# Attention of batches 3 to 7 spread over 1.4 instead of 1.6 pairs of a mixer kernel, with a fourth pair by seven products

## The chip, the core and the metric

The kernel runs on one core of a Trainium2 chip. The core has a matrix engine (PE), a vector engine (DVE), a scalar engine for activations (ACT), a general engine (POOL) and an engine that mostly issues DMA transfers (SP). Each takes its instructions in order and waits for the others by semaphores. The metric is the device time of one execution in microseconds; it was 559.47 us before (median of three runs, 558.79 to 559.52).

## What is computed

Normalised attention over 8 batches of 12 heads (448 positions, 64 columns a head), then a low-rank mix over positions, then a two-layer network of 768, 3072 and 768 columns:

```python
q_n, k_n = rmsnorm(q, g_q), rmsnorm(k, g_k)
scores = scale * np.matmul(q_n, k_n.transpose(0, 1, 3, 2))
attn = np.exp(scores - max); attn = attn / (sum(attn) + 1e-09)
x = (attn @ v).transpose(0, 2, 1, 3).reshape(B, S, H * D)

h = x.transpose(0, 2, 1) @ U @ V
u = x + h.transpose(0, 2, 1)
out = u + np.maximum(u @ w_ch1, 0.0) @ w_ch2
```

## The kernel before, in words

**Tiles of positions.** The 8 x 448 positions are 28 tiles of 128. A ring `xr` of ten tiles (`NX`, line 106) holds x, and a ring `ur` of four (`NU`) holds u turned around. Tiles 0 to 2 go through the network together (`mlp_first`), tile 3 alone (`mlp_single`), tiles 4 to 27 by pairs (`mlp_pair`, g = 1 to 12; pair g has tiles 2g+2 and 2g+3).

**A pair.** The first layer (`ph`, line 648) takes 144 products of 256 columns: 24 column blocks of `w1b`, six partial products each. Each bank of results is evicted through `relu` into `hT`, two times of three by ACT (line 430), else by DVE (line 432). The second layer (`po`, line 521) is always made of seven block products in the manner of Strassen and Winograd, 84 products of 384 columns, on sums of blocks of `hT` (DVE, line 529) and of `w2b` (kept in `comb`).

**A late pair.** From pair `LATE` on (10 before) the first layer too is made of seven products (`products_late`, line 572): seven times 36 products of 128 columns. They run in words like `10 50 11 20 60 51 21 70 30 ...`; the first digit is the product, the second which third of the 12 column blocks it makes, and a word is 12 products. Products 1 and 5 open banks of their own; ACT copies product 1's bank into a further bank, to which 6 and 7 add. After 6 a DVE addition (line 609) reads this bank, and after 7 another one (line 611). They need sums of blocks of `w1b`: R1 = V21 + V22, R2 = R1 - V11, R3 = V11 - V21 (written over V21), R4 = V12 - R2, 12 pieces each, all on DVE (line 548), and four sums of u (`sums_u`, into the tile E0). Product 5 uses R1, 6 uses R2, 7 uses R3, 3 uses R4. `held`, in the tile E1, takes intermediate results. So the first late pair can't begin before the last attention has let go of E0 and E1.

**Attention.** Twelve heads of a batch are six head pairs p (48 in all, `NP`). For a head pair: load raw q and k (fp32), squares (ACT, line 236), sums over columns (`reduce`, DVE, line 241), the reciprocal root (`rsqrt`, ACT, lines 246 and 247, for two head pairs at a time), scaling to bf16 (`scale`, POOL, line 256), a transpose by DMA into `qkT` (SP, line 286), then scores (PE, line 304), exponentials (ACT, line 313), the product with v (PE, line 320) and the division by the row sums (DVE, lines 335 to 348). Scores run in sessions of three, eight sessions a batch. Squares are made four head pairs ahead of the scores, scaling and transpose two ahead.

**Raw q and k.** A load covered two head pairs (`load(t)`, four transfers), into one of two buffers `qkL` of 2048 columns. In the steady part it was issued at every second head pair, behind the transpose of the second one.

**The order of the work.** It is all written out by hand. `step` takes the next piece of network work (`fill`) and, each time, one pending DVE sum, or two from the list `slack` when none is pending. `weave` puts attention pieces between, by weights, so that they are spread evenly up to a given place of the network:

```python
for b in range(2, B):
    end = 1.557 + 1.6 * (b - 2)
    weave(fill, stage(end), attention(b))
    weave(fill, stage(end + 0.257), mixing(b))
```

A place of 3.5 is half through pair 3, counted in PE columns; the first layer is the first 0.533 of a pair. Attention of batch 7 so ended at 9.557, just past the first layer of pair 9. `mixing` makes u of a batch and turns it into `ur` by DMA (`turn_u`), which waits for a place in the ring where there is none. At the start of a late pair, what is pending is issued and `slack` is emptied down to 12 pieces; the rest goes on two a step, at the latest ahead of the words of product 7.

Of the kernel before, what the change touches and what calls it, by code (L numbers as in the profile page):

```python
# [10 lines left out]
FP32 = mybir.dt.float32  # L11
BF16 = mybir.dt.bfloat16
# [6 lines left out]
def kernel(  # L19
# [83 lines left out]
    vas = [v[0:SP] for v in vw]  # L103


    NX, NU = 10, 4
    xr = consts.tile([P, NX, dm], BF16, name="xr")
    ur = consts.tile([P, KD, NU * P], BF16, name="ur")
    zero = xr[:, NX - 1]
    qkTs = [consts.tile([P, SQK + 16], BF16, name=f"qkT{i}") for i in range(NQ)]  # L110
    qkL = [consts.tile([P, 2, 2, 2, NJ * D], FP32, name=f"qk{i}") for i in range(2)]
    vL = consts.tile([P, HG, NJ * D], FP32, name="vt")
    part = consts.tile([P, HALF], FP32, name="part")

# [8 lines left out]
    def as_v(x):  # L123
        return x.rearrange("p (h c) -> p h c", h=HG)

    qk_of = {2: spare[:, 0:2048].rearrange("p (a s h c) -> p a s h c", a=2, s=2, h=2)}
    v_of = {0: as_v(slot(4)), 1: as_v(slot(5)), 2: as_v(spare[:, 2048:3072]), 4: as_v(slot(4)), 5: as_v(slot(5)),
            7: as_v(slot(5))}
    for t in range(NT):
        qk_of.setdefault(t, qkL[(t - (t > 2)) % 2])  # L130
        v_of.setdefault(t, vL)

    def setup():
# [62 lines left out]

    def load_pair(eng, t, s, a, hs=slice(0, 2)):
        rows, src = heads((q, k)[s], HG * t + 2 * a + hs.start, hs.stop - hs.start)
        eng.dma_start(qk_of[t][0:rows, a, s, hs], src)

    def load(t):
        for a in range(2):
            for s in range(2):
                load_pair(nc.sync, t, s, a)

    def load_v(t):
        rows, src = heads(v, HG * t, HG)
# [1 line left out]

    def touch(t):  # L210

        nc.vector.memset(qk_of[t][0:1, :, :, 0, 0:1], 0.0)
        nc.vector.memset(v_of[t][0:1, 0, 0:1], 0.0)

    def cast_v(t):
        nc.gpsimd.tensor_copy(vas[t % NV][:, :, :, 0:D], v_of[t][0:SP].rearrange("p h (j d) -> p h j d", d=D))

    def new_sq():
        return norm.tile([P, 2 * 2 * NJ * D], FP32, tag="sq", name="sq", bufs=1)

    def new_qkn():
        return norm.tile([P, NJ, 4, D], BF16, tag="qkn", name="qkn", bufs=2)
# [1 line left out]
    ALL = slice(0, 2)  # L224

    def squares(p, eng="pool", hs=ALL):
        t, a = divmod(p, 2)
        if 2 <= p < 6:
            sqs[p] = w2b[0:SP, 1].rearrange("p k n -> p (k n)").bitcast(FP32)[:, (p - 2) * 1024:(p - 1) * 1024]
        elif p < 16 and p not in sqs:  # L230
            sqs[p] = slot(p % 4 if p > 5 else p)[0:SP]
        elif p not in sqs:
            sqs[p] = new_sq()[0:SP]
        src, dst = qk_of[t][0:SP, a, :, hs], sqs[p].rearrange("p (s h c) -> p s h c", s=2, h=2)[:, :, hs]
        if eng == "act":
            nc.scalar.activation(dst, src, AF.Square)  # L236
        else:
            nc.gpsimd.tensor_tensor(dst, src, src, OP.mult)
# [8 lines left out]
        nc.scalar.activation(rs, rs, AF.Exp, scale=-0.5)  # L247

    def scale(p, pool=False):
        t, a = divmod(p, 2)  # L250
        qkns[p] = new_qkn()[0:SP]
        out = qkns[p].rearrange("p j g d -> p g j d")
        x = qk_of[t][0:SP, a].rearrange("p s h (j d) -> p (s h) j d", d=D)
        rs = rs_of(p).rearrange("p (g j) -> p g j ()", j=NJ)
        for g in (slice(0, 2), slice(2, 4)) if p >= 12 else (slice(0, 4),):
            (nc.gpsimd if p >= 12 or pool else nc.vector).tensor_tensor(  # L256
                out[:, g], x[:, g], rs[:, g].to_broadcast([SP, g.stop - g.start, NJ, D]), OP.mult)
# [270 lines left out]
    def later(fn, *args):  # L528
        pending.append(lambda: fn(*args))  # L529

    LATE = 10
    wq = w1b.rearrange("p (d i) (k j n) -> p j d k i n", d=2, j=2, n=P)
    Q = KH // 2
    V11, V12, V21, V22 = ([wq[:, j, d, k] for k in range(Q)] for j in range(2) for d in range(2))
# [5 lines left out]
    def pieces(tile_, names, dtype=FP32):  # L540
        x = tile_.rearrange(names)
        x = x.bitcast(BF16) if dtype == FP32 else x
        n = x.shape[1] // (KD // 2 * P)
        return [x[:, i * KD // 2 * P:(i + 1) * KD // 2 * P].rearrange("p (i n) -> p i n", n=P) for i in range(n)]

    def spread(fn, outs, xs, ys, op):
        for o, x, y in zip(outs, xs, ys):
            slack.append(lambda o=o, x=x, y=y: fn(o, x, y, op))

    def sums_first():  # L550
        R1.extend(pieces(qkL[1], "p a s h c -> p (a s h c)") + pieces(vw[0], "p h j d -> p (h j d)", BF16))
        spread(nc.vector.tensor_tensor, R1, V21, V22, OP.add)

    def sums_rest():
        qn = [pieces(new_qkn(), "p j g d -> p (j g d)", BF16) for _ in range(2)]
        R2.extend(pieces(qkL[0], "p a s h c -> p (a s h c)") + qn[0])
        R4.extend(pieces(vL, "p h c -> p (h c)") + pieces(new_sq(), "p c -> p c") + qn[1])
        assert [len(x) for x in (R1, R2, R4)] == [Q] * 3
        spread(nc.vector.tensor_tensor, R2, R1, V11, OP.subtract)
        spread(nc.vector.tensor_tensor, R4, V12, R2, OP.subtract)  # L560

    def quarter(u, d, a):
# [71 lines left out]
    def mlp_pair(g):  # L634
# [8 lines left out]
        for k in range(KH // 2 if g < LATE else 0):  # L643
            ph = ps_mm.tile([P, 4, P], FP32, tag="mm", name="ph")
            for j in range(2):
                hc, out = 2 * k + j, ph[:, 2 * j:2 * j + 2].rearrange("p a n -> p (a n)")
                for dc in range(KD):
                    nc.tensor.matmul(out, w1b[:, dc, hc * P:(hc + 1) * P], u[:, dc, :],  # L648
                                     start=(dc == 0), stop=(dc == KD - 1))
                if j == 0:  # L650
                    yield 2 * P
            relu(hB[:, 0:4, k, :], ph, k % 3 or g > 8)
            if g == 1 and k in (1, 4, 7, 9):
                later(combine, 12 + (1, 4, 7, 9).index(k))
            if k % 4 == 3:
                sums_h(k // 4)
            yield 2 * P
# [71 lines left out]
    def attention(b):  # L729
# [19 lines left out]
        for p in range(b * 6, b * 6 + 6):  # L749
            t, odd = divmod(p, 2)  # L750
            early = p < 12
            if p == 12:
                add(0, gains, p)
            run(p, 0)
            if p == NP - 4:
                add(0, sums_first)
            elif p == NP - 2:
                add(0, sums_rest)
            if p == 11:
                add(0, touch, 7)  # L760
                add(0, load, 7)
                add(0, load_v, 7)
            elif p >= 13 and p + 3 < NP:
                add(0, reduce, p + 3)
            elif early and odd:
                add(0, rsqrt, p + 1, 2)
                add(0, scale, p + 1)
            elif early and p > 6:
                add(0, scale, p + 1)
            run(p, 1)  # L770
            if not odd and p >= 14 and p + 2 < NP:
                add(0, rsqrt, p + 2, 2)
            if p >= 12 and p + 2 < NP:
                add(0, scale, p + 2)
                add(0, dma_transposes, p + 2)
            if p % 6:
                add(1, values, p - 1, 0)
            if p == 11:
                add(0, reduce, 12)
            if early and not odd:  # L780
                add(0.5, transposes, p + 1)
                if p < 10:
                    add(0, reduce, p + 2)
            if p + 1 < NP and p > 11:
                add(0, gains, p + 1)
            run(p, 2)
            if p % 6:
                add(1, values, p - 1, 1)
            if early and not odd:
                if p < 10:  # L790
                    add(0, reduce, p + 3)
                for a in range(2):
                    if p != 8:
                        add(0, squares, (10 if p == 6 else 12) + a)
            if p >= 12 and t + 2 < NT:
                add(0, squares, p + 4, "act")
            if odd and p > 11:
                if t + 3 < NT:
                    add(0, load, t + 3)
                if t + 2 < NT:  # L800
                    add(0, load_v, t + 2)
            if not odd and t + 1 < NT:
                add(0, cast_v, t + 1)
            run(p, 3)
            if early and odd and p < 11:
                add(1, transposes, p + 1)
            if p == 9:
                add(0, touch, 6)
                add(0, load, 6)
                add(0, load_v, 6)  # L810
# [68 lines left out]
    def head():  # L879
# [15 lines left out]
            return held[key].rearrange("p (s j r) -> p s j r", s=2, j=NJ)  # L895

        def raw0(s):
            return qk_of[0][0:SP, 0, s].rearrange("p h (j d) -> p j h d", d=D)

        def op(name, p, n, how):  # L900
            if name == "sq":
# [100 lines left out]
    with tc.manual_schedule():  # L1002
# [55 lines left out]
        for a in range(2):  # L1058
            reduce(14 + a)
        rsqrt(14, 2)  # L1060
        load(8)
        while at[0] < place("single", 0):
            step(fill)
        def stage(x):
# [1 line left out]
            return begins["ph", g][0] + (x - g) * (begins["ph", g + 1][0] - begins["ph", g][0])  # L1066

        for b in range(2, B):
            end = 1.557 + 1.6 * (b - 2)
            weave(fill, stage(end), attention(b))  # L1070
            weave(fill, stage(end + 0.257), mixing(b))
        while step(fill) is not None:
            pass
# [30 lines left out]
```

## Time and profile before

| | |
|---|---|
| median of three runs | 559.47 us |
| the profiled execution | 559.42 us |
| its span in the trace | 557.6 us |
| granted clock of PE | 0.999 |
| first layer of plain pairs (line 648) | 1296 products of 256 columns |
| second layer (line 521) | 1032 products |
| first layer of late pairs (line 595) | 756 products of 128 columns |
| DVE sums for late pairs (line 548) | 48 |
| exponentials (line 313) | 174.9 us busy on ACT |
| loads of q and k on SP after the first | 44 and 44, median 4.3 and 4.8 us to landing |
| transposes qkT by DMA | 36, median 3.1 us to landing |

A line of the page's groups has the source line, the engine, the operation, the tiles (result, then operands), the shape and the number; then busy time, mean length of one, and idle time of the engine before it with what ended it. A matmul's own length overlaps its neighbours', since products are pipelined; the pace of a row of products is its length in the chain of waits over its number. Windows give for one stretch of the span the busy time of each engine. In a view in order of time the first column is the start, the second the length, and what stands in brackets is the idle time before it and its releaser.

### The profile page before, as it was taken

How to read it: one execution, taken by the hardware profiler on the slowest of the kernel's cores; microseconds unless marked ns; L12 is line 12 of the kernel's file. 1: busy time of each engine (PE TensorE's matmuls, PEld its weight loads, DVE VectorE, ACT ScalarE, POOL GpSimd, SP SyncE). 2: the span in 40 equal slices, each digit the busy share in tenths (PEclk: the TensorE clock that was granted, in tenths of full speed). 3: DMA queues.
4: the chain of work that ended last, by engine and by line, in shares of the span. 5: the costliest groups of instructions: out<-in, count | busy, mean ns of one | idle time of the engine just before them, and what ended most of it. 6: DMA issues, size and time to landing. Idle time of an engine off the chain costs nothing.

```text
span 557.6 us, 13969 instructions
## 1 busy us (share of the span) xinstructions
PE 547.9 (98%) x5796; PEld 387.4 (69%) x5798; DVE 375.3 (67%) x834; ACT 318.1 (57%) x539; POOL 174.0 (31%) x171
## 2 busy tenths in 40 slices
PE   8999999999999999999999999999999999999996
PEld 3665665767768577577676686786776777878785
DVE  6977858388667657755676667556759778565654
ACT  7966640688458653678178654786185731515140
POOL 6964127434153230444244502424134100000000
PEclk9999999999999999999999999999999999999999
DMA  8999997946548553675165651668331403110101
GB/s 277 282 237 241 204 238 203 207 134 179 130 91 166 140 120 111 165 163 145 55 127 152 154 166 45 188 130 168 93 77 37 75 2 85 31 58 2 58 2 57
DMA packets 108447, 72.43 MB, mean 130 GB/s; under 512 B 56688, under 2 KB 105056, under 8 KB 108384
## 3 DMA queue, kind: packets, MB, share of 16 engines
q1 hardware_dynamic: 96800, 61.65, 44.2%
q0 software_dynamic: 11008, 9.44, 10.5%
q8 instruction: 45, 0.74, 0.6%
q10 hardware_dynamic: 576, 0.46, 0.3%
q14 instruction: 18, 0.15, 0.1%
HBM read 56.78 MB, written 11.01 MB: 122 GB/s over the span
## 4 chain that ended last, share of the span: by engine, by line
PE 88%; DVE 5%; ACT 3%; issue 1%; DMA 1%; SPq 1%; POOL 0%; DVEq 0%; POOLq 0%
PE po L521 28%; PE ph L648 24%; PE o L320 8%; PE po L476 5%; PE sc L304 4%; PE ph L595 4%; PE ph L458 3%; PE sc L595 3%; PE sh L304 3%; ACT E L313 2%; PE px L397 1%; DMA qk<-in_k_dram 1%; PE ph L486 1%; DVE hT L529 1%; PE bank L320 1%
## 5 line engine op out<-in xcount | busy, mean ns | idle before, releaser
L648 PE MATMUL ph<-ur,w1b 128*128 128x256 bf16 x1296 | 156.0, 273 | 0.0
L521 PEld LDWEIGHTS <-hT 128*128 128x128 bf16 x1032 | 95.9, 98 | 63.2 <-issue 7.2
L648 PEld LDWEIGHTS <-w1b 128*128 128x128 bf16 x1296 | 121.8, 98 | 25.9 <-issue 10.8
L256 POOL TENSOR_TENSOR qkn<-qk,rms 112x512 bf16<-112x512 f32 (+1 forms) x73 | 83.0, 1157 | 152.4 <-ACT rms L247 111.5
L313 ACT ACTIVATE E<-sc 112x896 bf16<-112x896 f32 x138 | 122.0, 920 | 2.2 <-PE sc L304 2.1
L521 PE MATMUL po<-w2b,hT 128*128 128x384 bf16 (+1 forms) x588 | 104.2, 323 | 0.0
L430 ACT ACTIVATE hT<-ph 128x512 bf16<-128x512 f32 (+1 forms) x101 | 58.9, 586 | 71.1 <-PE ph L648 63.8
L529 DVE TENSOR_TENSOR hT<-hT 128x512 bf16<-128x512 bf16 x144 | 73.2, 527 | 17.3 <-ACT hT L430 15.4
L313 ACT ACTIVATE E<-sh 112x448 bf16<-112x448 f32 x108 | 52.9, 543 | 55.9 <-PE sh L304 55.8
L521 PE MATMUL po<-comb,hT 128*128 128x384 bf16 (+1 forms) x444 | 78.5, 322 | 0.0
L320 PEld LDWEIGHTS <-E 112*128 112x128 bf16 x1536 | 60.7, 98 | 10.2 <-issue 2.9
L694 POOL TENSOR_TENSOR osb<-osb,xr 128x384 f32<-128x384 f32 x12 | 11.9, 992 | 152.5 <-DVE osb L693 147.4
L320 PE MATMUL o<-va,E 112*128 112x65 bf16 x1344 | 57.1, 194 | 0.3 <-DVE hT L432 0.2
L335 DVE RECIPROCAL rec<-o 128x4 f32<-128x4 f32 x84 | 15.0, 179 | 48.8 <-PE o L320 48.6
L432 DVE TENSOR_SCALAR hT<-ph 128x512 bf16<-128x512 f32 (+1 forms) x51 | 33.8, 663 | 19.6 <-PE ph L648 17.2
L241 DVE TENSOR_REDUCE sums<-sq 112x16 f32<-112x1024 f32 x32 | 38.7, 1208 | 4.6 <-ACT sq L236 4.5
L304 PE MATMUL sc<-qkT 64*128 64x448 bf16 x268 | 39.1, 351 | 1.3 <-DVE qkT L275 0.6
L399 DVE TENSOR_TENSOR xr<-px,xr 128x384 bf16<-128x384 f32 x56 | 29.9, 551 | 8.1 <-PE px L397 5.1
L476 PE MATMUL po<-w2b,hT 128*128 128x384 bf16 x192 | 34.5, 326 | 0.1
L236 ACT ACTIVATE sq<-qk 112x1024 f32<-112x1024 f32 x32 | 33.9, 1059 | 0.0
L304 PEld LDWEIGHTS <-qkT 64*128 64x128 bf16 x376 | 14.8, 94 | 25.9 <-issue 15.3
L344 DVE TENSOR_TENSOR xr<-o,rec 128x192 bf16<-128x192 f32 (+1 forms) x96 | 30.8, 331 | 2.9
(154 smaller groups left out, 605.8 us busy)
## 6 DMA issues: line engine op xcount, KB each, us to landing
qk<-in_q_dram SPq DMA_DIRECT2D x44, 256.0 KB, 4.3
qk<-in_k_dram SPq DMA_DIRECT2D x44, 256.0 KB, 4.8
vt<-in_v_dram SPq DMA_DIRECT2D x17, 512.0 KB, 6.0
w1b<-in_moe_w_ch_dram POOLq DMA_DIRECT2D x6, 768.0 KB, 20.6
w2b<-in_moe_w_ch_dram POOLq DMA_DIRECT2D x6, 768.0 KB, 36.6
comb<-in_v_dram SPq DMA_DIRECT2D x5, 512.0 KB, 9.0
out_dram<-osb SPq DMA_DIRECT2D x7, 336.0 KB, 3.1
out_dram<-osb SPq DMA_DIRECT2D x7, 288.0 KB, 2.9
```

What stands on the lines that cost most here:

```text
L236: nc.scalar.activation(dst, src, AF.Square)
L241: nc.vector.tensor_reduce(rs_of(p, of=sums).rearrange("p (s h j) -> p s h j", s=2, h=2)[:, :, hs], sqs[p].rearrange("p (s h j d) -> p s h ...
L256: (nc.gpsimd if p >= 12 or pool else nc.vector).tensor_tensor(out[:, g], x[:, g], rs[:, g].to_broadcast([SP, g.stop - g.start, NJ, D]), OP ...
L304: nc.tensor.matmul(sc[hh][0:n, 0:S], flat[pp, c:c + n], blocks(p)[pp, :, 0], start=True, stop=True)
L313: nc.scalar.activation(dst, src, AF.Exp, scale=float(D) ** 0.5)
L320: nc.tensor.matmul(o[:, i, :], E[:, c:c + P], va[:, hl, kc, :], start=(kc == 0), stop=(kc == NJ - 1))
L430: nc.scalar.activation(out, ph, AF.Relu)
L476: nc.tensor.matmul(po, left(hc), w2b[:, half, hc, :], start=(hc == 0), stop=(hc == KH - 1))
L521: nc.tensor.matmul(bank, left[:, k, :], right[:, k, cols], start=start and k == 0, stop=k == KH // 2 - 1, skip_group_check=not start)
L529: pending.append(lambda: fn(*args))
L595: nc.tensor.matmul(to[:, j * P:(j + 1) * P], left[4 * n + j][:, i], right[:, i], start=m in (1, 5) and j == 0 and i == 0, stop=i == KD // ...
L648: nc.tensor.matmul(out, w1b[:, dc, hc * P:(hc + 1) * P], u[:, dc, :], start=(dc == 0), stop=(dc == KD - 1))
```

## The change

Six parts, which belong together:

- `LATE` goes from 10 to 9: pair 9 makes its first layer by seven products too. The pair that is evicted by ACT alone becomes pair 8, and pair 8's last sums go from POOL to DVE.
- Batches 3 to 7 end 1.4 instead of 1.6 pairs after one another; batch 7 ends at 8.557 instead of 9.557. Batch 2 keeps its end at 1.557.
- Ten x tiles become twelve.
- Raw q and k are held by head pairs in three buffers of 1024 columns (`qkP`), some early ones in other tiles. In the steady part each head pair's load (two transfers) is issued at head pair p for p + 5, right behind the transpose of p + 2.
- R1 and R2 lie in the three raw buffers, in `vt` and in the `qkn` tiles, and their sums begin at the last head pair but one; R4 lies in `sq` and in parts of E0 and E1, and its sums are put on the list when batch 7's attention is woven in, behind R3's.
- The tile of zeros for the first warming products is x tile 10 instead of 9.

```diff
-    NX, NU = 10, 4
+    NX, NU = 12, 4
-    zero = xr[:, NX - 1]
+    zero = xr[:, 10]
-    qkL = [consts.tile([P, 2, 2, 2, NJ * D], FP32, name=f"qk{i}") for i in range(2)]
+    qkP = [consts.tile([P, 2, 2, NJ * D], FP32, name=f"qk{i}") for i in range(3)]
...
+    sq0 = as_qk(new_sq())
+    raw = {0: qkP[0], 1: qkP[1], 2: qkP[2], 3: as_qk(slot(3)), 4: as_qk(spare[:, 0:1024]),
+           5: as_qk(spare[:, 1024:2048]), 6: qkP[0], 7: qkP[1], 8: qkP[2], 9: sq0, 10: qkP[0], 11: qkP[1],
+           12: qkP[2], 13: sq0}
+    for p in range(14, NP):
+        raw[p] = qkP[(p + 1) % 3]
...
+    def load_one(p):
+        for s in range(2):
+            load_pair(nc.sync, p // 2, s, p % 2)
...
     def touch(t):
-        nc.vector.memset(qk_of[t][0:1, :, :, 0, 0:1], 0.0)
+        for a in range(2):
+            nc.vector.memset(raw[2 * t + a][0:1, :, 0, 0:1], 0.0)
...
-    LATE = 10
+    LATE = 9
...
     def sums_first():
-        R1.extend(pieces(qkL[1], "p a s h c -> p (a s h c)") + pieces(vw[0], "p h j d -> p (h j d)", BF16))
+        qn = [pieces(new_qkn(), "p j g d -> p (j g d)", BF16) for _ in range(2)]
+        qk = [pieces(x, "p s h c -> p (s h c)") for x in qkP]
+        R1.extend(qk[0] + qk[1] + qn[0])
+        R2.extend(qk[2] + pieces(vL, "p h c -> p (h c)") + qn[1])
         spread(nc.vector.tensor_tensor, R1, V21, V22, OP.add)
+        spread(nc.vector.tensor_tensor, R2, R1, V11, OP.subtract)
 
     def sums_rest():
-        qn = [pieces(new_qkn(), "p j g d -> p (j g d)", BF16) for _ in range(2)]
-        R2.extend(pieces(qkL[0], "p a s h c -> p (a s h c)") + qn[0])
-        R4.extend(pieces(vL, "p h c -> p (h c)") + pieces(new_sq(), "p c -> p c") + qn[1])
+        U = KD // 2 * P
+        R4.extend(pieces(new_sq(), "p c -> p c") + pieces(Ew[0][:, 4 * U:9 * U], "p c -> p c", BF16)
+                  + pieces(Ew[1][:, 2048:2048 + 2 * U], "p c -> p c", BF16))
-        spread(nc.vector.tensor_tensor, R2, R1, V11, OP.subtract)
         spread(nc.vector.tensor_tensor, R4, V12, R2, OP.subtract)
...
-            relu(hB[:, 0:4, k, :], ph, k % 3 or g > 8)
+            relu(hB[:, 0:4, k, :], ph, k % 3 or g == LATE - 1)
...
-            if p == NP - 4:
+            if p == NP - 2:
                 add(0, sums_first)
-            elif p == NP - 2:
-                add(0, sums_rest)
...
                 add(0, scale, p + 2)
                 add(0, dma_transposes, p + 2)
+                if p + 5 < NP:
+                    add(0, load_one, p + 5)
...
             if odd and p > 11:
-                if t + 3 < NT:
-                    add(0, load, t + 3)
                 if t + 2 < NT:
                     add(0, load_v, t + 2)
...
-        load(8)
+        load_one(16)
...
-            end = 1.557 + 1.6 * (b - 2)
+            end = 1.557 + 1.4 * (b - 2)
             weave(fill, stage(end), attention(b))
+            if b == B - 1:
+                sums_rest()
             weave(fill, stage(end + 0.257), mixing(b))
```

## The prediction

> **What bounds the kernel now.** I read the page's busy times, then the chain of waits, then windows over the attention stages, then single engines in order of time.
>
> ```profile
> PE 547.9 (98%) x5796; PEld 387.4 (69%) x5798; DVE 375.3 (67%) x834; ACT 318.1 (57%) x539; POOL 174.0 (31%) x171
> ```
>
> Busy share does not show whether PE runs at its pace, so I read the chain next (start, length, what):
>
> ```profile
> 355.80 3.28 PE ph L648 x30
> ...
> 497.84 2.68 PE ph L595 x48
> ...
> 513.86 11.70 PE po L521 x72
> ```
>
> This gives three paces without a gap: a 256-column product of the plain first layer takes 3.28/30 = 109.3 ns, a 128-column product of the seven-product form 2.68/48 = 55.8 ns, a 384-column second-layer product 11.70/72 = 162.5 ns. A plain pair is thus 144 x 109.3 + 84 x 162.5 = 15.74 + 13.65 = 29.39 us. PE sets the time as long as nobody is late for it.
>
> The windows run over the eight score sessions of batches 2 to 6 (stretch, length, then busy PE, PEld, DVE, ACT, POOL with counts, clock, DMA share, GB/s):
>
> ```profile
> 102.70:139.10 36.40, 35.75 (x438) 26.47 (x436) 26.29 (x52) 31.52 (x53) 16.57 (x14) 1.00 0.69 180
> 158.40:199.50 41.10, 41.10 (x411) 28.62 (x410) 26.04 (x53) 31.91 (x53) 16.52 (x16) 1.00 0.60 130
> 219.90:261.30 41.40, 41.40 (x417) 28.96 (x416) 25.18 (x53) 32.34 (x55) 19.03 (x17) 1.00 0.57 138
> 281.00:321.90 40.90, 40.90 (x417) 29.04 (x416) 27.06 (x60) 32.59 (x55) 18.94 (x17) 1.00 0.59 139
> 342.90:384.00 41.10, 41.10 (x413) 28.63 (x412) 25.45 (x55) 31.75 (x53) 18.61 (x17) 1.00 0.59 130
> ```
>
> Batches 3 to 6 leave PE no idle time, with ACT at 77 to 80%. Batch 2, which the change leaves as it is, is closer packed: ACT 87%, PE idle 0.65 us.
>
> The last views are DVE and PE where the first seven-product pair begins (its first product starts at 469.52):
>
> ```profile
> 470.12 0.55 DVE L722 TENSOR_TENSOR osb<-po,osb 128x384 f32<-128x384 f32 x1
> 470.58 1.15 DVE L548 TENSOR_TENSOR w1b<-w1b 128x384 bf16<-128x384 bf16 x4
> 473.57 0.70 DVE L609 TENSOR_TENSOR ph<-sc,E 128x512 f32<-128x512 f32 x1 [1.84 <-PE sc L595]
> ```
>
> ```profile
> 472.63 0.83 PE L595 MATMUL sc<-E,qk 128*128 128x128 bf16 x12
> 473.30 0.83 PE L595 MATMUL ph<-E,qk 128*128 128x128 bf16 x12
> 473.97 0.83 PE L595 MATMUL ph<-ur,w1b 128*128 128x128 bf16 x12
> 474.64 0.83 PE L595 MATMUL sc<-E,w1b 128*128 128x128 bf16 x12
> ```
>
> The reader is to see that DVE has 1.84 us to spare before L609. L609 adds up bank sc after product 6 of the first third (PE at 472.63), and product 7 (PE at 474.64) writes the same bank, so PE may not start it before L609 has read.
>
> **The change part by part.** The sum starts from the profiled execution's own 559.42 us (span 557.6); the median of the runs is 559.47, so both are the same here.
>
> *Fourth pair by seven products.* It takes 144 products away and puts 7 x 36 = 252 in: 252 x 55.8 = 14.07 us for 15.74, which is -1.67 us on PE. In this kernel PE's time is the span's.
>
> By the Trainium skill ("TensorE: Matmul & The Clock Gate", section "Back-to-back issue gap") this should not pay: it puts a sustained stream of weight load and matmul at about 81 ns for 128 columns, an estimate of 20.4 us for the 252. The trace has 55.8 ns for just this stream in three pairs, and the sum goes by the trace.
>
> *The sums for it.* R1, R2, R3 and R4 are 12 DVE additions each, as before. But R4 now lies in the two E tiles and so waits until batch 7's attention is done, and R3 has by then been put into the list ahead of it. In the built program's order DVE, after pair 8's last eviction (L722 before), has 6 sums of R3 and all 12 of R4 ahead of its first L609; before it had 4 of R3 alone. From the view above: eviction from 470.12, sums from 470.58, 1.15/4 = 0.287 us each. Eighteen take 5.17, so L609 would run from 475.75 to 476.45, and product 7, which stood at 474.64, waits 1.8 us. PE is in order: the rest of the first layer is queued behind it. After that the two are as far apart as before. Bounds: 0, if DVE comes there earlier than I think (it can't come before the eviction, which needs PE's last product, so this takes sums of half the length), and 2.2 us at the 0.35 us of some sums. I take 1.75.
>
> *Batches 3 to 7 at 1.4.* Attention of a batch was spread over 1.6 - 0.257 = 1.343 pairs and gets 1.143: 0.2 x 29.39 = 5.9 us less fill over 8 sessions, 0.73 us each. Sessions stood 41.15/7 = 5.88 us apart in batch 3 (first exponentials at 158.77 and 199.92) and come to about 5.15. Batch 2 has 36.57/7 = 5.22. So batch 2 is what the others become: about 31 us of ACT in 36, 87%. It pays 0.65 us of PE idle, nearly all in one place (PE's next score bank waits for ACT's L430) and while the single tile's evictions, all on ACT, run. A pair gives ACT two evictions of three. Price per batch 0 to 0.65, for five batches 0 to 3.2 us; nearest is the 0 of batches 3 to 6 for most sessions, so I take 0.16 each, 0.8 us. A gain is possible only in batch 7, whose attention has 0.23 us idle now.
>
> *Raw q and k by pairs.* As many loads (two a pair) on SP's queue, but each pair's are issued right behind the transpose of the pair whose buffer they refill. That transpose waits for POOL's scaling, which waits for ACT's rms. At even pairs the squares of the loaded pair on ACT come soon after. From rows: rms ends at 161.02 and the squares one pair-step on begin at 171.30, so 10.3 us, and about 9 us at the new density (1.75 sessions x 0.73 less). Needed: POOL 2.25, SP's transpose 1.25, two load issues 1.03, landing 4.8 (page, k), gaps about 0.2: 9.5 us. ACT would then wait some 0.5 us at about 13 places, with the exponentials of that session queued behind, for which PE's next session waits. ACT at 87% idles 0.13 x 5.15 = 0.67 us a session, so a wait of 0.5 us is mostly covered where that idle time lies next to it. Uncovered it is 13 x 0.6 = 7.8 us. I take 0.8, between 0 and 7.8, nearer to the covered end.
>
> *At nothing.* Twelve x tiles: batch 5's split of one normalisation goes, batch 3 gets one, the same 96 instructions. Two memsets more (60 ns each on DVE), beside PE work. R1 no longer has pieces in va (two sums of 1.1 us there with POOL busy beside); DVE's, not PE's time. Pair 8 instead of pair 9 is evicted by ACT alone and summed by DVE: the same place relative to batch 7's end. The head keeps its order, its loads the same places on SP. Uncovered, any of these is below 0.3 us.
>
> Sum: 559.42 - 1.67 + 1.75 + 0.8 + 0.8 = 561.1 us.
>
> **The rivals.**
> *The gain stands (faster).* The eighteen sums are not late and batches 3 to 7 stay without idle: 559.42 - 1.67 = 557.75. For it: PE idle 0 in four batches and ACT 13% free at the new density. Against it: 18 sums in program order ahead of L609.
> *Gain and sums cancel, the rest is covered (no change).* 559.42 + 0.08 = 559.5. For it: batch 2 idles at one place only; against: every even pair's chain is longer than its time.
> *ACT decides.* From 5.2 us between sessions all five batches pay batch 2's idle: 561.1 + 2.4 = 563.5.
> *Loads decide.* Loads land after ACT is there; half the uncovered price shows: 561.1 - 0.8 + 3.9 = 564.2. It decides once the landing passes 5 us; DMA share is 0.69 in batch 2, 0.6 elsewhere.
> *Weight loads set the pace of the new products.* At the 98 ns of one LDWEIGHTS, 252 take 24.7 us, 9.0 more than the plain layer: 568.4 with nothing else. Three pairs at 55.8 ns speak against it. This is the skill's rule above, made a bound.
> That the fourth pair does not change form is excluded by the built program: 1008 products of 128 columns for 756.
>
> **How the numbers follow.** Forecast 0.34, gain stands 0.21, cancel 0.21, ACT 0.12, loads 0.11, weight loads 0.01. Runs of this kernel can't tell less than 0.2% (1.1 us) from no change, so 558.35 and 560.59 are the limits: faster 0.21; no change 0.21 and the lower edge of the forecast, 0.24; slower the rest, 0.55. The forecast's own range is 560.3 to 562.6. The range of 8 in 10 goes down to the gain standing and up past the two slower cases: 557.6 to 564.8.
>
> **What would show it.** Pair 9's first layer: 252 products at 56 ns with one hole of 1.5 to 2 us ahead of product 7 of its first third, put down to DVE, and 18 sums in a row on DVE just before. No hole: that step was wrong. PE idle in windows over sessions of batches 3 to 7: 0.1 to 0.3 us each; over 0.6, ACT decides. Squares on ACT that wait for a DMA of q or k at even pairs: nought to 0.6 us. If PE loses nothing in these three places, the time is 557.8 and the prediction wrong; if it loses elsewhere (scores waiting for a transpose, x or u tiles late), the accounting is.

## The result, and the profile after

The changed kernel takes 563.97 us (median of four runs, 563.34 to 564.82), against 559.40 before beside it: a ratio of 1.0085 [1.0067, 1.0102], 4.6 us slower. In a second set of runs it took 565.34 (564.00 to 565.59), 1.0095 [1.0078, 1.0113]. The profiled execution took 564.11 with a span of 562.3.

The page's busy times, of after (busy time, share, instructions):

```profile
PE 548.0 (97%) x5906; PEld 388.4 (69%) x5906; DVE 373.7 (66%) x847; ACT 321.4 (57%) x546; POOL 172.4 (31%) x170
```

PE is as busy as before (547.9) in a span 4.7 us longer. So the loss is idle time of PE, which the busy shares cannot place.

The windows over the eight score sessions of batches 2 to 7, of after (stretch, length, then busy PE, PEld, DVE, ACT, POOL with counts, clock, DMA share, GB/s):

```profile
103.40:139.90 36.50, 35.85 (x439) 26.53 (x438) 26.40 (x52) 31.63 (x53) 16.16 (x14) 1.00 0.73 173
159.50:195.20 35.70, 35.17 (x375) 25.21 (x372) 21.76 (x55) 31.40 (x53) 15.08 (x14) 1.00 0.62 149
215.70:252.00 36.30, 35.44 (x366) 24.50 (x362) 21.60 (x48) 29.73 (x51) 18.28 (x16) 1.00 0.57 147
270.00:306.00 36.00, 36.00 (x382) 25.50 (x380) 23.39 (x51) 29.34 (x50) 17.23 (x16) 1.00 0.58 145
326.00:362.00 36.00, 35.89 (x375) 25.00 (x374) 22.22 (x49) 30.16 (x52) 14.61 (x14) 1.00 0.57 146
383.90:420.00 36.10, 34.11 (x356) 23.26 (x353) 19.00 (x50) 26.60 (x48) 14.36 (x12) 1.00 0.39 85
```

The stretches are now 36 us long, as batch 2's was, and ACT is busy 81 to 88% in batches 2 to 6. But PE's idle time does not follow from that: 0.53, 0.86, 0.00, 0.11 and 1.99 us in batches 3 to 7. Batch 7, where ACT has the least to do (74%), loses the most.

The waits of PE, of after (who waits for whom, us in total, times, longest), those that the profile of before does not have:

```profile
PE po L531 <- ACT hT L440: 1.7, 1, 1.7
PE sc L608 <- DVE ph L622: 1.4, 1, 1.4
...
PE ph L661 <- ACT hT L440: 0.7, 1, 0.7
...
PE sc L314 <- ACT qkT L301: 0.5, 1, 0.5
```

(Lines have moved: exponentials are L323, evictions L440, transposes of gains L301, squares L247, scaling L266, the second layer L531, the first layer of plain pairs L661 and of late ones L608, DVE's sums L558 and the addition after product 6 L622.) Four waits stand for most of the loss. Each happens once; they are single places, and not a steady lack of an engine.

*The first* is in pair 7. ACT and PE there, each engine's timeline of after (start, length, engine, line, out<-in, count, and the idle time before it with its releaser):

```profile
383.98 0.97 ACT L323 ACTIVATE E<-sh 112x448 bf16<-112x448 f32 x2
384.82 0.93 ACT L323 ACTIVATE E<-sc 112x896 bf16<-112x896 f32 x1
385.62 0.34 ACT L257 ACTIVATE rms<-sums,eps 112x32 f32<-112x32 f32 x1
386.00 0.23 ACT L258 ACTIVATE rms<-rms 112x32 f32<-112x32 f32 x1
386.13 0.65 ACT L301 ACTIVATE qkT<-qkT,gg 128x448 bf16<-128x448 bf16 x1
386.69 0.90 ACT L323 ACTIVATE E<-sc 112x896 bf16<-112x896 f32 x1
387.49 1.04 ACT L247 ACTIVATE sq<-qk 112x1024 f32<-112x1024 f32 x1
388.43 0.58 ACT L440 ACTIVATE hT<-ph 128x512 bf16<-128x512 f32 x1
```

```profile
385.38 1.95 PE L531 MATMUL po<-w2b,hT 128*128 128x384 bf16 x11
389.07 0.34 PE L531 MATMUL po<-w2b,hT 128*128 128x384 bf16 x1 [1.75 <-ACT hT L440]
```

Batch 7 now begins at place 7.414, with pair 7's first layer ending at 7.533. Its first session puts 4.4 us of work on ACT with no gap in it, and the last eviction of pair 7's first layer stands at the end of that queue. PE, which is in order too, runs the second layer up to the product that needs this eviction and stops for 1.75 us. How little decides this is seen in before: its batch 4 began at the same place of a pair, 3.414, and had the same burst. ACT's timeline of before:

```profile
220.52 0.97 ACT L313 ACTIVATE E<-sh 112x448 bf16<-112x448 f32 x2
221.37 0.93 ACT L313 ACTIVATE E<-sc 112x896 bf16<-112x896 f32 x1
222.16 0.34 ACT L246 ACTIVATE rms<-sums,eps 112x32 f32<-112x32 f32 x1
222.54 0.23 ACT L247 ACTIVATE rms<-rms 112x32 f32<-112x32 f32 x1
222.67 0.65 ACT L291 ACTIVATE qkT<-qkT,gg 128x448 bf16<-128x448 bf16 x1
223.23 0.57 ACT L430 ACTIVATE hT<-ph 128x512 bf16<-128x512 f32 x1
```

There the eviction stood two instructions further ahead, before the next exponential (0.90) and the squares (1.04), and PE lost 0.16 us.

*The second* is the one that was forecast, ahead of product 7 in pair 9. DVE, then PE, of after:

```profile
445.55 0.55 DVE L735 TENSOR_TENSOR osb<-po,osb 128x384 f32<-128x384 f32 x1
446.01 1.70 DVE L558 TENSOR_TENSOR w1b<-w1b 128x384 bf16<-128x384 bf16 x6
447.62 1.43 DVE L558 TENSOR_TENSOR sq<-w1b,qk 128x384 bf16<-128x384 bf16 x5
448.96 1.44 DVE L558 TENSOR_TENSOR E<-w1b,vt 128x384 bf16<-128x384 bf16 x5
450.30 0.63 DVE L558 TENSOR_TENSOR E<-w1b,qkn 128x384 bf16<-128x384 bf16 x2
450.84 0.70 DVE L622 TENSOR_TENSOR ph<-sc,E 128x512 f32<-128x512 f32 x1
```

```profile
449.41 0.83 PE L608 MATMUL ph<-ur,w1b 128*128 128x128 bf16 x12
451.60 0.83 PE L608 MATMUL sc<-E,w1b 128*128 128x128 bf16 x12 [1.36 <-DVE ph L622]
```

Six sums of R3 (into `w1b`) and twelve of R4 (into `sq` and E) run behind the eviction, and only then the addition for which product 7 waits. A word of 12 products starts 0.67 us after the one before; here it is 2.19, so the hole costs 1.52 us.

*The third* is at the start of batch 4: a first-layer product waits 0.70 us for ACT, where again an eviction stood behind a burst of 4.4 us (215.69 to 220.15). The end of the burst on ACT, then PE:

```profile
219.20 1.04 ACT L247 ACTIVATE sq<-qk 112x1024 f32<-112x1024 f32 x1
220.15 1.07 ACT L440 ACTIVATE hT<-ph 128x512 bf16<-128x512 f32 x2
```

```profile
220.78 2.78 PE L661 MATMUL ph<-ur,w1b 128*128 128x256 bf16 x24 [0.70 <-ACT hT L440]
```

*The fourth* is at the start of batch 3: scores wait 0.53 us for ACT to multiply `qkT` with the gains, and ACT had waited 1.37 us for the DMA transpose:

```profile
168.41 0.67 ACT L301 ACTIVATE qkT<-qkT,gg 128x448 bf16<-128x448 bf16 x1 [1.37 <-DMA qkT<-qkn]
169.13 0.36 PE L314 MATMUL sc<-qkT 64*128 64x448 bf16 x2 [0.53 <-ACT qkT L301]
```

The transpose waits for POOL's scaling, and POOL was late. Its timeline of after:

```profile
161.61 1.81 POOL L726 TENSOR_TENSOR osb<-osb,part 128x768 f32<-128x768 f32 x1 [3.97 <-DVE part L719]
163.38 2.05 POOL L266 TENSOR_TENSOR qkn<-qk,rms 112x512 bf16<-112x512 f32 x2
```

A last addition of pair 1 stands ahead of the scaling on POOL, which so begins 1.6 us after ACT's reciprocal root is ready (161.77).

The same addition stood ahead of the same scaling in before (160.87, then 162.64), at no loss. There the scores that needed the transpose began 10.5 us behind the batch's first exponential; here they begin 8.5 us behind it.

What PE lost, place by place, is read from the starts of its products against the paces of the prediction (what a stop costs until the pace is there again, so slightly more than the idle time shown):

| place | us |
|---|---|
| fourth pair by seven products, 252 for 144 | -1.67 |
| start of batch 7, eviction of pair 7 late | +1.91 |
| pair 9, product 7 | +1.52 |
| start of batch 4, eviction of pair 3 late | +0.85 |
| start of batch 3, scaling late | +0.69 |
| eight holes of 0.19 to 0.40 (sum 2.14), for five in before (1.17) | +0.97 |
| the head of this execution was longer | +0.75 |
| sum | +5.0, of 4.7 |

The entry on the head is this execution's own. One and the same early score product starts at 47.49 us in it, at 46.70 in before and at 46.40 in a later profile of the same changed kernel; over all twelve profiles here it starts between 45.88 and 47.49. A difference of two profiled spans therefore has up to 1.6 us of the head in it.

### The profile page after: what moved, and what is told of

Read it like the earlier page. It is cut to its first block, busy times and chain, and to the rows that moved or that the text cites. A ratio compares the mean times of both kernels' runs of the same rounds, so it can differ in the third digit from the quotient of the medians.

```text
span 562.3 us, 14194 instructions
## 1 busy us (share of the span) xinstructions
PE 548.0 (97%) x5906; PEld 388.4 (69%) x5906; DVE 373.7 (66%) x847; ACT 321.4 (57%) x546; POOL 172.4 (31%) x170
## 4 chain that ended last, share of the span: by engine, by line
PE 83%; ACT 6%; DVE 4%; DMA 2%; issue 2%; POOL 1%; SPq 0%; DVEq 0%; POOLq 0%; ACTq 0%
PE po L531 27%; PE ph L661 19%; PE o L330 7%; PE po L486 5%; PE ph L608 5%; PE sc L314 4%; PE sc L608 4%; ACT E L323 3%; PE ph L468 3%; PE sh L314 3%; PE px L407 1%; DMA comb<-in_q_dram 1%; ACT hT L440 1%; ACT sq L247 1%; PE ph L496 1%
## 5 line engine op out<-in xcount | busy, mean ns | idle before, releaser
L661 PE MATMUL ph<-ur,w1b 128*128 128x256 bf16 x1152 | 140.4, 273 | 0.7 <-ACT hT L440 0.7
L531 PEld LDWEIGHTS <-hT 128*128 128x128 bf16 x1032 | 96.1, 98 | 64.8 <-issue 6.1
L661 PEld LDWEIGHTS <-w1b 128*128 128x128 bf16 x1152 | 107.8, 98 | 23.4 <-issue 9.6
L323 ACT ACTIVATE E<-sc 112x896 bf16<-112x896 f32 x138 | 122.0, 920 | 2.2 <-PE sc L314 2.1
L266 POOL TENSOR_TENSOR qkn<-qk,rms 112x512 bf16<-112x512 f32 (+1 forms) x71 | 79.8, 1144 | 133.3 <-ACT rms L258 77.8
L531 PE MATMUL po<-w2b,hT 128*128 128x384 bf16 (+1 forms) x588 | 104.4, 323 | 1.7 <-ACT hT L440 1.7
L440 ACT ACTIVATE hT<-ph 128x512 bf16<-128x512 f32 (+1 forms) x96 | 56.2, 588 | 62.8 <-PE ph L661 55.4
L539 DVE TENSOR_TENSOR hT<-hT 128x512 bf16<-128x512 bf16 x144 | 68.4, 493 | 17.8 <-ACT hT L440 16.2
L323 ACT ACTIVATE E<-sh 112x448 bf16<-112x448 f32 x108 | 52.9, 544 | 45.6 <-PE sh L314 45.4
L531 PE MATMUL po<-comb,hT 128*128 128x384 bf16 (+1 forms) x444 | 77.2, 322 | 0.0
L707 POOL TENSOR_TENSOR osb<-osb,xr 128x384 f32<-128x384 f32 x12 | 14.4, 1198 | 186.1 <-DVE osb L706 177.5
L608 PEld LDWEIGHTS <-w1b 128*128 128x128 bf16 x576 | 34.3, 98 | 3.1 <-issue 1.5
L618 ACT COPY sc<-ph 128x512 f32<-128x512 f32 x12 | 6.8, 570 | 51.1 <-PE ph L608 35.5
L247 ACT ACTIVATE sq<-qk 112x1024 f32<-112x1024 f32 x32 | 33.8, 1057 | 0.5 <-DMA qk<-in_k_dram 0.4
```

Source lines behind the costliest of these rows:

```text
L323: nc.scalar.activation(dst, src, AF.Exp, scale=float(D) ** 0.5)
L440: nc.scalar.activation(out, ph, AF.Relu)
L531: nc.tensor.matmul(bank, left[:, k, :], right[:, k, cols], start=start and k == 0, stop=k == KH // 2 - 1, skip_group_check=not start)
L608: nc.tensor.matmul(to[:, j * P:(j + 1) * P], left[4 * n + j][:, i], right[:, i], start=m in (1, 5) and j == 0 and i == 0, stop=i == KD // ...
```

## The experiments

Each ran beside before on the same chip, and its ratio is to before.

**The order of the sums.** R4 goes on the list ahead of R3 (both in `sums_rest`), and R3's last eight are held back.

```diff
-    pending, slack = [], []
+    pending, slack, kept = [], [], [0]
...
+        spread(nc.vector.tensor_tensor, R3, V11, V21, OP.subtract)
+        kept[0] = 8
...
-        if g == LATE - 1:
-            spread(nc.vector.tensor_tensor, R3, V11, V21, OP.subtract)
...
-            for _ in slack[:2]:
+            for _ in slack[:min(2, max(0, len(slack) - kept[0]))]:
```

> The changed kernel with R4's sums put ahead of R3's on the list and the last eight of R3 kept back until the words of product 7, so that DVE has 10 sums instead of 18 between pair 8's last eviction and the first addition after product 6. My step (the 18 sums cost PE 1.5 us at the start of pair 9): the hole of 1.36 us ahead of product 7 goes, the time falls by 1.4 to 1.6 us, to about 562.5. Rival (the hole belongs to the first late pair in any case, from bank reuse): it stays and the time stays at 564.0.

It took 566.51 (1.0127 [1.0096, 1.0157]): slower than after, a miss. The hole ahead of product 7 was gone, but a larger one had come. PE's timeline of this run:

```profile
444.67 0.83 PE L610 MATMUL ph<-ur,w1b 128*128 128x128 bf16 x12
448.01 0.38 PE L619 MATMUL sc<-w1b 128*128 128x512 bf16 x1 [2.51 <-DVE w1b L558]
```

L619 is a product whose result nobody uses; it opens the bank of product 1's copy. It reads the first 512 columns of `w1b`, blocks of V21 that R3's first sums overwrite, and with R4 first it came behind them. The edit made a wait of its own. So it went in again with this product reading `comb`, and with the held sums let go after the first addition:

```diff
-                    nc.tensor.matmul(Qb[n], w1b[:, 0, 0:P], w1b[:, 0, 0:512], start=True, stop=True)
+                    nc.tensor.matmul(Qb[n], w1b[:, 0, 0:P], comb[:, 0].rearrange("p k n -> p (k n)")[:, 0:512], start=True, stop=True)
...
                 nc.vector.tensor_tensor(Zb[n], Qb[n], keep, OP.add)
+                kept[0] = 0
```

> The first experiment again without the wait that its edit brought in: there PE stood 2.5 us at the matmul that opens the bank of product 6 (it reads columns of w1b that R3's first sums overwrite, and these had come late). It now reads a block of comb, and the rest of R3 is let go after the first addition. 10 sums instead of 18 stand ahead of that addition. My step: no hole over 0.3 us at the start of pair 9, 562.4 for the changed kernel's 564.0. Rival (some other condition holds PE there): a hole of over 1 us stays and the time does not fall.

562.89 (1.0061 [1.0049, 1.0074]). PE's timeline of this run, product 6 and then product 7:

```profile
448.83 0.83 PE L610 MATMUL ph<-ur,w1b 128*128 128x128 bf16 x12
449.50 0.83 PE L610 MATMUL sc<-E,w1b 128*128 128x128 bf16 x12
```

Product 7 follows at the pace. A hole of 0.41 us is left at 451.5, where product 4 waits for the addition after 7, which eight sums of R3 precede. So the hole of 1.52 us came from the order of the eighteen sums, and the mended order leaves 0.41 of it. The median fell by 1.1, which fits; by the intervals it is 1.1 give or take 1.2, so the traces show this and the times alone do not.

**The last eviction of pair 7.** DVE takes it instead of ACT.

```diff
-            relu(hB[:, 0:4, k, :], ph, k % 3 or g == LATE - 1)
+            relu(hB[:, 0:4, k, :], ph, k % 3 and not (g == 7 and k == 11) or g == LATE - 1)
```

> The changed kernel with the last first-layer bank of pair 7 evicted by DVE instead of ACT. The trace has PE waiting 1.75 us there for ACT's eviction, which stands behind 4.4 us of work that the start of batch 7 puts on ACT. If that queue is the cause: the hole goes and the time falls by 1.7 to 1.9 us, to about 562.1. Rival (PE would have waited for batch 7's scores or for ACT's copy of part a moment later anyway): the hole moves, the time falls by less than 0.5 us.

561.50 (1.0039 [1.0019, 1.0059]), 2.5 us below after (give or take 1.5), by one eviction moved; 1.7 to 1.9 were expected. PE's timeline of this run at the place where after has 1.75 us idle:

```profile
385.45 2.11 PE L531 MATMUL po<-w2b,hT 128*128 128x384 bf16 x12
387.50 0.36 PE L314 MATMUL sh<-qkT 64*128 64x448 bf16 x2
```

The twelve products run through. The eviction's place in ACT's queue was the cause, shown.

**Three pairs, closer attention kept** (`LATE = 10`, 1.4 as in the change).

> The changed kernel with LATE back at 10: closer attention, pair buffers and twelve x tiles, but no fourth pair by seven products (and so R4's sums long before pair 10). If the closer attention carries the loss: 1.67 us of gain go, 1.5 us of hole go, the time stays within 0.4 us of the changed kernel's 564.0, and the holes at the starts of batches 3, 4 and 7 are still there. Rival (the fourth pair and its sums carry the loss): close to the 559.4 of before.

564.38 (1.0085 [1.0061, 1.0109]), as slow as after. The waits of PE in this run:

```profile
PE po L531 <- ACT hT L440: 1.8, 1, 1.8
...
PE ph L661 <- ACT hT L440: 0.7, 1, 0.7
...
PE sc L314 <- ACT qkT L301: 0.5, 1, 0.5
```

The same three places, without the one in pair 9. Fourth pair and sums together are worth 563.97 - 559.40 less 564.38 - 559.63, which is -0.2 us, give or take 1.7 by the intervals; the table's -1.67 + 1.52 gives -0.15.

**The buffers alone** (`LATE = 10`, 1.6 instead of 1.4, and R4 ahead of R3 on the list). The first form had the wait of the first experiment in it (2.13 + 0.40 us at the same products), so that its 563.62 (1.0066 [1.0044, 1.0087]) gives no verdict on buffers:

> The changed kernel with LATE at 10 and the attention 1.6 pairs apart, with the sums' order of the first experiment: only the raw pairs in three buffers, their loads behind the transposes, and twelve x tiles are left of the change. If these cost nothing: 559.4 as before, within 0.3 us. If the 0.75 us that the changed kernel lost in the first 13 us of its profile belong to the buffers: 560.2. If the loads come late even at the old spacing: 561 or more, with ACT waiting for q and k.

With the mended order:

```diff
-    LATE = 9
+    LATE = 10
...
-            end = 1.557 + 1.4 * (b - 2)
+            end = 1.557 + 1.6 * (b - 2)
```

> The fourth experiment again with the same mending: raw pairs in three buffers, their loads and twelve x tiles, at 1.6 pairs and with three late pairs. Its profile with the 2.5 us of the edit's own holes was 2.5 us above before. If buffers and loads cost nothing: 559.6, within 0.5 us of before. If they cost what the fourth experiment's median had over its own profile: 561 or more.

559.92 (1.0031 [1.0002, 1.0059]), 0.4 us above before, and its profiled execution 558.91, half a microsecond below before's. The interval is wide, 0.1 to 3.3 us, since two of the eleven executions took 565.7 and 566.8. In the trace every wait of PE of 0.5 us or more stands in before's too, and the mended order's hole of 0.41 is added. So at the old spacing three raw buffers by pairs, their loads and twelve x tiles cost about 0.4 us by the median, and nothing that the trace shows.

**The two other places.** Pair 1's last additions go from POOL to DVE, and DVE evicts one more bank of pair 3.

```diff
-            relu(hB[:, 0:4, k, :], ph, k % 3 or g == LATE - 1)
+            relu(hB[:, 0:4, k, :], ph, k % 3 and not ((g, k) == (3, 7)) or g == LATE - 1)
...
-        if LATE - 1 <= g and not last:
+        if (LATE - 1 <= g or g == 1) and not last:
```

> The changed kernel with two edits at the starts of batches 3 and 4: pair 1's last additions on DVE instead of POOL, so that POOL scales 1.8 us earlier and the transpose for the session at 168 us is there in time; and one bank of pair 3's first layer (block 7) evicted by DVE instead of ACT. If the bursts at batch starts are the cause: the holes of 0.69 and 0.86 us go, the time falls by 1.5 us to 562.4. Rival (something else is late right behind): at least one hole stays over 0.4 us.

561.59 (1.0048 [1.0035, 1.0060]), 2.4 us below after. The hole of 0.85 is gone, that of 0.69 is 0.22. POOL's scaling in this run begins 0.1 us after the reciprocal root is ready, where after has 1.6:

```profile
160.66 2.45 POOL L266 TENSOR_TENSOR qkn<-qk,rms 112x512 bf16<-112x512 f32 x2 [4.25 <-ACT rms L258]
```

The holes add up to 1.3 us less. The profiled execution fell by 2.5: the other 1.3 is its head, where the early score product named above starts at 46.19. That the median fell by 2.4 (give or take 1.2) is not explained beyond the holes.

**All four edits together.**

> The changed kernel with all four edits: sums in the other order, pair 7's last eviction on DVE, and the two of the run before. If the holes are independent: 564.0 - 1.5 - 1.9 - 1.5 = 559.1, within 0.7 us, so level with before or a little under it, and the fourth pair's 1.67 us is what pays for the small holes left. Rival (PE-bound work moves on to the next late engine): 560.5 or more.

558.92 (0.9992 [0.9983, 1.0001]), span 556.9 in the profiled execution: 5.05 us below after and level with before. The windows over batches 3 and 7 of this run:

```profile
159.50:195.20 35.70, 35.62 (x378) 25.28 (x377) 23.87 (x59) 30.75 (x53) 13.67 (x13) 1.00 0.64 150
...
383.90:420.00 36.10, 35.85 (x385) 24.90 (x384) 22.61 (x60) 28.07 (x47) 14.56 (x12) 1.00 0.41 85
```

PE idles 0.08 and 0.25 us there, for 0.53 and 1.99 in after. A last form, which keeps the held sums back also through the second third's first words, aimed at the hole of 0.41:

```diff
-                kept[0] = 0
+                kept[0] = 0 if n else kept[0]
```

> The run with all four edits, with the eight last sums of R3 let go only after the second addition of product 6. The 0.41 us hole that was left in pair 9 (product 4 waits for the addition after product 7, which stood behind these eight sums) goes, the other small holes stay: 558.9 - 0.4 = 558.5, by its ratio just below before. If the eight sums are late for product 7's later thirds instead, the hole only moves and the time stays at 558.9.

559.03 (0.9987 [0.9966, 1.0008]), no difference that can be told. The hole is 0.2 at another place.

**The changed kernel once more**, beside the last one:

> The changed kernel itself, once more. Its first profile began its first-layer work 0.8 us later than before, as none of the experiments did. If that was this one execution: the same holes from 100 us on, a head like before's, and 563 to 564. If it belongs to the change: the 0.8 us are there again.

565.34, as given above. The four large holes are there again.

## Why the prediction was right or wrong

The direction was right, the time was 2.9 us too low, and one term carries the error.

- *What bounds.* PE at its pace, and every stop of PE is the time: right. Taking the stop of 1.91 us away moved the profiled execution by 1.8 and the median by 2.5, more than its length, which stays unexplained.
- *Gain of the fourth pair, -1.67.* Its 252 products ran at 0.67 us for 12, the forecast pace, and three pairs in place of four left the time where it was, within 1.7 us, once the sums' hole is set against it. Right, by the trace. By the Trainium skill ("TensorE: Matmul & The Clock Gate", section "Back-to-back issue gap") 12 of them would take 0.97 us, an estimate from its 81 ns for one; the words of 12 in pair 9 start 0.67 apart, so the trace does not bear that out here.
- *Eighteen sums, +1.75.* 1.52 measured, at the product and behind the instruction that were named, and the mended order of the sums takes it away. Right.
- *Closer attention, +0.8.* This is the step that failed, by its size: "nearest is the 0 of batches 3 to 6 for most sessions, so I take 0.16 each, 0.8 us". By the experiments it is 564.38 - 559.63 less 559.92 - 559.48, so 4.3 us, give or take 2; by the table 1.91 + 0.85 + 0.69 + 0.97, so 4.4. For the two largest parts, 1.91 + 0.85, the mechanism named was the right one (ACT's queue filled, PE waiting for an eviction at its end); the 0.69 came through POOL, which the term did not have. But I priced it as a share: idle time per batch, from batch 2. It came mostly as three single stops, where an eviction fell behind the burst of a batch's first session, or a scaling behind a POOL addition. Batches 5 and 6, as closely spaced as the others, lost 0.00 and 0.11. Nor did the bound of 3.2, five times batch 2's idle time, hold it: one stop alone took 1.91.
- *Loads of raw q and k, +0.8.* Wrong, and nearly nothing. ACT's squares in after (busy, mean ns of one, and idle time ahead with its releasers):

```profile
L247 ACT ACTIVATE sq<-qk 112x1024 f32<-112x1024 f32 x32 | 33.8, 1057 | 0.5 <-DMA qk<-in_k_dram 0.4
```

They waited 0.4 us in all, not 0.5 at each of 13 places. In the later profile of the same kernel it was 1.1, and in the run of the four edits 0.2. The run of the buffers alone, at the old spacing, has 0.4 us by its median. The loads landed in 3.4 and 3.6 us (median) where I had used 4.8. By the same sum that takes the 9.5 us down to about 8.3, under the 9 that there were. And 13 places at 0.5 us make 6.5, not the 7.8 of the upper end.
- *"At nothing".* Twelve x tiles and the pieces in other tiles: the run of the buffers alone shows no wait for them. What that list lacks is the order of POOL's additions behind pair 1: the change leaves it alone, but the closer attention needs the scaling behind it sooner, 0.69 us. The prediction's last sentence had this as a sign that its accounting was wrong (scores waiting for a transpose).

Of the rivals, "Loads decide" (564.2) is nearest in time and has the wrong reason: the squares hardly waited for loads. "ACT decides" (563.5) is next. By the sign set for it, PE idle over 0.6 us in the windows, it holds in batches 4 and 7; but its reason was that all five batches pay, and batches 5 and 6 paid nearly nothing, while batch 7, with ACT at 74%, lost most. "The gain stands" came true only in part and only with the four edits: they end 0.5 us under before, [-0.95, +0.06] by its ratio's interval, where 1.67 was to be had. The rest lies in holes of 0.2 to 0.4 us each, which none of the runs took apart; nor was it tried to place the starts of the batches unevenly instead of moving evictions.

## What to carry to other kernels

When work is packed closer, don't price it by an engine's free share: list, for each place where a burst begins, what stands behind it on the same in-order engine, and whether the bottleneck needs that next. Here one eviction behind 4.4 us of a burst cost more than the whole change could gain, and giving it to the engine next door brought it back. And before putting back an order by hand, look up who else reads what the reordered work overwrites, down to products whose result is not used.

## What was not expected of the hardware

A stop of 1.75 us was not always paid off when it ended. In the second profile of the changed kernel, PE took up its products after the hole at 387 and then ran at about half its clock. Windows of PE and the other engines, of that second profile and then of the first, over the same time:

```profile
390.00:392.00 2.00, 2.00 (x9) 0.99 (x8) 2.00 (x3) 2.00 (x4) 1.54 (x2) 0.57 0.82 191
392.00:394.00 2.00, 2.00 (x9) 1.02 (x8) 1.41 (x2) 0.83 (x2) 0.00 (x0) 0.58 1.14 266
```

```profile
390.00:392.00 2.00, 2.00 (x15) 1.21 (x14) 2.00 (x3) 2.00 (x4) 1.74 (x2) 1.00 0.86 192
```

The granted clock (third number from the end) is 0.57 for 1.00, and the twelve second-layer products behind the hole took 3.63 us instead of 2.12. Finer windows of the second profile place it: PE idles 1.75 us between 386.85 and 390.26, the clock is 0.50 from there to 393.67, and 1.00 again after. So a stretch of 3.41 us at half clock followed one of the same length that held the whole hole. The Trainium skill ("TensorE: Matmul & The Clock Gate", section "HAM oscillation — how this bites in real kernels") has it that idle gaps over about 3.4 us are to be avoided; here a gap of half that length went ahead of a fall of the clock in one of two profiled executions. The Trainium skill ("TensorE: Matmul & The Clock Gate", section "What's actually happening") also says that the window is free-running. That would fit a hole that is sometimes caught whole and sometimes cut in two; what the limit is, no run here shows, and no edit was made to test it.

Over the eight runs of the changed kernel, the three with a mean granted clock of 0.997 and one at 0.998 took 564.8 to 565.6, the four at 0.999 or 1.000 took 563.3 to 564.1: some 1.4 us more, which is the kernel's spread. A mean of 0.998 alone does not show such a fall. In before the 15 runs at 0.998 have a median of 559.38, the 20 at 1.000 one of 559.69; and the profile of the moved eviction, at 0.998, has a clock of 1.00 up to 558 us and 0.59 only behind that, where PE has nothing left to do. Means of 0.997 or less were in three of these eight runs, in one of 55 of before, and in none of 23 of the two forms with all four edits; but also in two of 11 of the buffers alone, which have none of the four holes. The fall of the clock explains little of why taking a hole away brought more than its length: without its one run at 0.997 the changed kernel's first median would be 563.82 for 563.97.
